# Attention decode with a gated FFN: K and V in four large units, K turned on VectorE

## The chip, the cores and the metric

The kernel runs on one core of a Trainium2 chip. The time is that of the device, in microseconds, from the first to the last instruction of the core; the median of the timed runs counts. The engines are TensorE (PE), VectorE (DVE), ScalarE (ACT), GpSimd (POOL) and SyncE (SP, which here only issues transfers). PEld is PE's loading of the stationary operand.

## What is computed

Two sequences of one token each (B = 2), model width 448, 16 query heads over 8 K/V heads of 256, and a window of the last 2048 keys of a cache of 8192:

```python
def reference(A_x, A_k_cache, A_v_cache, A_wq, A_wo, B_x, B_w1, B_w2):
    xn = _layernorm(A_x)                                  # [2, 1, 448]
    q = (xn @ wq) -> [2, 16, 1, 256]                      # wq 448 x 4096
    k, v = last W = 2048 rows of the caches, each head used by 2 query heads
    p = softmax(q k^T / 16);  o = p v                     # per sequence and head
    s = o -> [2, 1, 4096] @ wo                            # wo 4096 x 448
    g = silu(relu(xn @ w1) @ w2)                          # w1 448 x 1792, w2 1792 x 448
    return A_x + s * g
```

All inputs are bfloat16. K and V of the windows are 33.55 MB, wq and wo 3.67 MB each, w1 and w2 1.61 MB each.

## The kernel before

A small scheduler, `_Prog`, keeps one list of operations for each engine. Every list is executed strictly in the order in which the operations were added; dependences become semaphore waits. `run` writes the lists out inside an `nc.Block`, one body for each engine.

K and V come in 16 pieces each: one K/V head of one sequence, `[128 partitions x 16 keys x 256]`, 1 MB with rows of 8 KB (`kv_src`, L178). The pieces of K rotate through 6 buffers and those of V through 8; all are issued on SP in the order of the list at L463 to L475, behind wq and ahead of w1, w2 and wo (five parts, L481). A pair k is one head for both sequences.

- `do_T` (L260): PE transposes a chunk of K in four 128x128 f32 products (two bf16 values to an f32) into PSUM (L268); DVE (L278) and ACT (L280) in turn copy it to `kt`.
- `do_S` (L282): the scores of a pair, 16 products of 512 columns, four side by side in column tiles of the array; the moving operand steps 4 bytes.
- `ch_max`, `ch_rmT`, `ch_bias`, `ch_exp`, `ch_Pt`, `ch_sum` (L298 to L337): the softmax of a pair; maxima and P are transposed on PE.
- `do_PV` (L339), `do_osb` (L353), `do_oT` (L359): P times V in 32 products of 256 columns a pair, scaling, and folding into `at_exp`.
- `do_q` (L374) computes q from wq (28 products) and spreads it into `qz`.
- `do_H`, `do_hT`, `do_F` (L397 to L429): the FFN; H is twice seven products of 448 columns, one after the other, `do_F` 56 products of 112 columns and the sigmoid.

The table `steps` (L437 to L461) puts the parts of the pairs into one another: while K of pair k is transposed, the softmax and PV of pairs k-1 and k-2 run. FFN and output come after all pairs (L485 on): 128 products with wo (L498), two DVE operations (L503, L505), and two stores side by side on SP and ACT (L507), with a wait for both on SP.

Of the kernel before, what the change touches and what calls it, by code (L numbers as in the profile page):

```python
# [22 lines left out]
class _Prog:  # L23


# [14 lines left out]
    def run(self, block):  # L40
# [5 lines left out]
        for e, ops in self.lists.items():  # L46
            sem, count = self.es.enter_context(self.nc.semaphore(f"s_{e}")), 0
            for o in ops:
                if o.dma:
                    n += 1  # L50
                    o.sem, o.value = self.es.enter_context(self.nc.semaphore(f"d_{n}")), 16
                elif o.needed:
                    count += 1
                    o.sem, o.value = sem, count
# [16 lines left out]
        for name, e in (("gpsimd", POOL), ("sync", SP), ("scalar", ACTE), ("vector", DVE), ("tensor", PE)):  # L71
            def body(eng, ops=self.lists[e]):
                emit(eng, ops)
            getattr(block, name)(body)


def bass_recurrent_scan__sliding_block_cached__dense_activation_relu__decode_kernel(
# [21 lines left out]
    NT = W // 128  # L99
    NPAIR = HKV  # L100
    NCH = 8
    SLOTS = 7
    NKB = 6
    NVB = 8
    NKT = 12
    NP = 3
    HC = HD // 2
    FC = DFF // 2
    WO_PARTS = [10, 10, 8, 2, 2]
    NCOL = D // 4  # L110

    es = contextlib.ExitStack()
    with es:
# [8 lines left out]
        def view(t, off, dims, n=128, p0=0, pstep=1):  # L122
            width = t.shape[1]
            return bass.AP(t, p0 * width + off, [[width * pstep, n]] + dims)

        ident = named("ident", [128, 128], BF)
        ident_f = named("ident_f", [128, 128], F32)
        one_f = named("one_f", [128, 1], F32)
        par8 = named("par8", [128, 8], F32)
        par2 = named("par2", [128, 2], F32)  # L130
        qmask = named("qmask", [128, 4], F32)
        fold = named("fold", [128, 32], BF)
        gsum = named("gsum", [128, 128], F32)
        x_sb = named("x_sb", [128, D], BF)
        xg = named("xg", [128, 9 * 128], BF)
# [5 lines left out]
        q_n = named("q_n", [128, 512], BF)  # L141
        qz = named("qz", [128, 16 * NPAIR], BF)
        h_n = named("h_n", [128, FC], BF)
        h_sb = named("h_sb", [128, 28], BF)
        x_c = named("x_c", [128, NCOL], BF)
# [4 lines left out]
        rm = [named(f"rm{i}", [128, 1], F32) for i in range(2)]  # L150
        mrow = [named(f"mrow{i}", [128, 128], F32) for i in range(2)]
        bias = [named(f"bias{i}", [128, 1], F32) for i in range(2)]
        e_sb = [named(f"e_sb{i}", [128, 512], BF) for i in range(2)]
        ssum = [named(f"ssum{i}", [128, 1], F32) for i in range(2)]
        rs = named("rs", [128, NPAIR], F32)
        pt = [named(f"pt{i}", [128, 64], BF) for i in range(NP)]
        o_sb = [named(f"o_sb{i}", [128, 512], BF) for i in range(2)]
        at_exp = named("at_exp", [128, 256], BF)
        at2 = named("at2", [128, 64], BF)
# [4 lines left out]
        kbuf = [named(f"kbuf{i}", [128, NT * DH], BF) for i in range(NKB)]  # L164
        vbuf = [named(f"vbuf{i}", [128, NT * DH], BF) for i in range(NVB)]
        kt = [named(f"kt{i}", [128, 1024], BF) for i in range(NKT)]

        tb = [psum(f"tb{i}", [128, 1024], BF) for i in range(3)]
        sbk = psum("sbk", [128, 512], F32)
        fbk = psum("fbk", [128, 512], F32)  # L170
        obk = [psum(f"obk{i}", [128, 512], F32) for i in range(2)]
        mb16 = psum("mbk", [128, 1024], BF)
        mbk = mb16[:, :].bitcast(F32).tensor

        def mbk_ap(lo, n, rows=128):
            return view(mbk, lo, [[1, n]], n=rows)

        def kv_src(c, cache):  # L178
            hkv, b = divmod(c, 2)
            return cache[b, hkv, SK - W:SK, :].rearrange("(p t) d -> p (t d)", t=NT)  # L180

        d_x = pr.dma(ACTE, x_sb[0:B, :], A_x[:, 0, :])
        p_xc = pr.op(POOL, lambda e: e.memset(x_c[:, :], 0.0))
        d_xc = [pr.dma(ACTE, view(x_c, 0, [[1, NCOL]], n=4, p0=b, pstep=32),
                       A_x[b, 0, :].rearrange("(i n) -> i n", i=4), [p_xc]) for b in range(B)]
        d_k, d_v = {}, {}
        last_T, last_PV = {}, {}

        wq_src = A_wq.rearrange("r (hf c) -> (r hf) c", hf=2).rearrange("(p s) c -> p (s c)", s=SLOTS)
        w1_src = B_w1.rearrange("r (hf c) -> (r hf) c", hf=2).rearrange("(p s) c -> p (s c)", s=SLOTS)  # L190
        w2_src = B_w2.rearrange("(hf p j) n -> p hf (j n)", hf=2, j=7)
        wo_src = A_wo.rearrange("(p j) n -> p (j n)", j=32)

        def load_k(c):
            d_k[c] = pr.dma(SP, kbuf[c % NKB][:, :], kv_src(c, A_k_cache), [last_T.get(c - NKB)])

        def load_v(c):
            d_v[c] = pr.dma(SP, vbuf[c % NVB][:, :], kv_src(c, A_v_cache), [last_PV.get(c - NVB)])

        load_k(0)  # L200
        load_k(1)
        d_wq = pr.dma(SP, wqo[:, 0:SLOTS * HC], wq_src)
        load_k(2)
        load_k(3)
# [5 lines left out]
        i1 = pr.op(POOL, lambda e: e.memset(ident_f[:, :], 0.0), [p_id])  # L210
        p_idf = pr.op(POOL, lambda e: e.affine_select(
            out=ident_f[:, :], in_=ident_f[:, :], compare_op=ALU.not_equal, fill=1.0,
            base=0, pattern=[[-1, 128]], channel_multiplier=1), [i1])
        p_one = pr.op(POOL, lambda e: e.memset(one_f[:, :], 1.0), [p_idf])
        p_mr = [pr.op(POOL, lambda e, t=t: e.memset(t[0:1, :], 0.0)) for t in mrow][-1]
        p_qz = pr.op(POOL, lambda e: e.memset(qz[:, :], 0.0), [p_one])

        a_z = [pr.op(ACTE, lambda e, t=t: e.memzero(t[:, :])) for t in (obk[0], sbk, obk[1], fbk)]  # L218

# [4 lines left out]
        a_sd = pr.op(ACTE, lambda e: e.activation(sd[0:B, 1:2], sd[0:B, 0:1], ACT.Sqrt), [v_ve])  # L224
        v_rs = pr.op(DVE, lambda e: e.reciprocal(rstd[0:B, :], sd[0:B, 1:2]), [a_sd])
        for e2 in range(2):
# [5 lines left out]
        v_par = pr.op(DVE, lambda e: e.tensor_reduce(  # L232
            out=par2[:, :], in_=view(ident, 0, [[1, 2], [2, 64]]), axis=AX.X, op=ALU.add), [p_id])
        v_par8 = pr.op(DVE, lambda e: e.tensor_copy(
            view(par8, 0, [[2, 4], [1, 2]]), view(par2, 0, [[0, 4], [1, 2]])), [v_par])
        v_qm = pr.op(DVE, lambda e: e.tensor_reduce(
            out=qmask[:, :], in_=view(ident, 0, [[32, 4], [1, 32]]), axis=AX.X, op=ALU.add))

        def fold_op(e):
            with nc.allow_low_precision("zeros and ones"):  # L240
                return e.tensor_reduce(out=fold[:, :], in_=view(ident, 0, [[1, 32], [32, 4]]), axis=AX.X, op=ALU.add)
        v_fold = pr.op(DVE, fold_op)
        v_gs = pr.op(DVE, lambda e: e.tensor_copy(
            view(gsum, 0, [[32, 4], [1, 32]]), view(fold, 0, [[0, 4], [1, 32]])), [v_fold])
# [5 lines left out]
        for s in range(SLOTS):  # L250
            m_xr = pr.op(PE, mm(mbk_ap(2 * s, 2), xg[0:B, 128 * s + 128:128 * s + 256], ident[0:B, 0:B], s == 0),
                         [v_xn, p_id])
        v_xr = pr.op(DVE, lambda e: e.tensor_tensor(
# [3 lines left out]
        evac, last_S, freed = {}, {}, set()  # L257
        st = {}

        def do_T(i):  # L260
            k, s = divmod(i, NCH)
            c = 2 * k + s // 4
            bank, src = tb[i % 3], kbuf[c % NKB]
            src_f, bank_f = src[:, :].bitcast(F32), bank[:, :].bitcast(F32)
            deps = [d_k[c], p_idf, evac.get(i - 3)]
            for n in range(4):
                lo = (4 * (s % 4) + n) * (DH // 2)
                o = pr.op(PE, lambda e, n=n, lo=lo: e.matmul(  # L268
                    bank_f[:, n * 128:(n + 1) * 128], lhsT=src_f[:, lo:lo + 128], rhs=ident_f[:, :],
                    start=True, stop=True, is_transpose=True), deps)  # L270
                deps = []
            last_T[c] = o
            if s % 4 == 3:
                freed.add((load_k, c))
            dst = kt[i % NKT]
            deps = [o, last_S.get(i - NKT)]
            if i % 2 == 0:
                evac[i] = pr.op(DVE, lambda e: e.tensor_copy(dst[:, :], bank[:, :]), deps)  # L278
            else:
                evac[i] = pr.op(ACTE, lambda e: e.activation(dst[:, :], bank[:, :], ACT.Copy), deps)  # L280

        def do_S(k, b):  # L282
            bank = sbk
            deps = [st["q"], a_z[1]] + ([st["exp", k - 1]] if b == 0 and k else [])
            for dhi in range(2):
                lhsT = qz[:, 16 * k + 8 * dhi + 4 * b:16 * k + 8 * dhi + 4 * b + 4]
                for i in range(4):
                    ch = NCH * k + 4 * b + i
                    o = pr.op(PE, mm(bank[32 * i:32 * i + 4, :], lhsT,
                                     view(kt[ch % NKT], dhi, [[2, 512]]),  # L290
# [250 lines left out]
```

## Time and profile before

| what | value |
|---|---|
| median of three runs | 115.5 us (115.26 to 115.77) |
| the profiled execution, its span | 115.7 us |
| PE busy, instructions | 85.0 us (73%), 990 products |
| DVE busy | 49.4 us (43%), 131 instructions |
| ACT busy | 44.4 us (38%) |
| DMA read from HBM | 44.11 MB, 381 GB/s over the span |
| mean granted TensorE clock | 0.852 |
| first wo product, last DVE operation, end | 109.5, 113.0, 115.7 us |

The profile lists busy time by engine; a row of 40 digits for each engine, one digit for each 2.89 us, in tenths of busy time; the clock that TensorE was granted; the chain of work that ended last; and groups of like instructions with their mean duration, in nanoseconds, and the idle time before them with what ended it. Busy time of an engine that nobody waits for costs nothing.

### The profile page before, as it was taken

Reading aid. Unit: us, or ns where it says so; the run is one execution under the profiler, and the core shown is the slowest. Engines: PE = TensorE matmul, PEld = TensorE weight load, DVE = VectorE, ACT = ScalarE, POOL = GpSimd, SP = SyncE. Lnnn points to the kernel's source line nnn. Section 1 sums busy time; section 2 is a strip of 40 time slices with the busy share of each in tenths; the row PEclk is TensorE's granted clock in tenths of the full one; section 3 lists DMA queues with packets and bytes.
Section 4 is the critical chain, followed back from the end, with each engine's and each line's share of the span. In section 5 each row is a group of like instructions: output and inputs, shape, how many; then the busy total and the mean of one; then the engine's idle time right before and its main releaser. Section 6 shows DMA issues by size and latency. Waiting matters only on the chain.

```text
span 115.7 us, 2285 instructions
## 1 busy us (share of the span) xinstructions
PE 85.0 (73%) x990; PEld 53.7 (46%) x990; DVE 49.4 (43%) x131; ACT 44.4 (38%) x57; POOL 1.9 (2%) x13
## 2 busy tenths in 40 slices
PE   0009946980499799759989966999998695886390
PEld 0009923650275465428556544756665342225280
DVE  2046424560027456523745742565575524113401
ACT  1951650668024834813384380348465010000000
POOL 6000000000000000000000000000000000000000
PEclk9999999997559999985999998599999955555559
DMA  2998989999999999999999999999999999999200
GB/s 60 428 486 387 476 374 428 422 425 416 419 428 422 414 431 416 414 422 425 416 408 433 414 419 428 414 419 431 416 411 433 435 409 411 421 422 389 73 6 3
DMA packets 5934, 44.26 MB, mean 383 GB/s; under 512 B 674, under 2 KB 932, under 8 KB 1316
## 3 DMA queue, kind: packets, MB, share of 16 engines
q1 hardware_dynamic: 5896, 44.11, 91.7%
q8 instruction: 8, 0.13, 0.5%
q14 instruction: 2, 0.02, 0.0%
q10 hardware_dynamic: 28, 0.00, 0.0%
HBM read 44.11 MB, written 0.00 MB: 381 GB/s over the span
## 4 chain that ended last, share of the span: by engine, by line
DMA 46%; PE 38%; DVE 6%; ACT 4%; issue 1%; POOL 1%; POOLq 0%
DMA kbuf<-in_A_k_cache_dram 46%; PE tb L268 13%; PE fbk L247 10%; PE obk L247 6%; PE sbk L247 3%; PE mbk L247 3%; PE mbk L325 2%; ACT L224 1%; ACT L218 1%; DVE xg L227 1%; DVE h_n L404 1%; ACT obk L218 1%; DVE o_sb L355 1%; DVE tmp L427 1%; DVE rm L299 1%
## 5 line engine op out<-in xcount | busy, mean ns | idle before, releaser
L268 PE MATMUL tb<-ident_f,kbuf 128*128 128x128 f32 x256 | 43.7, 307 | 9.8 <-DMA kbuf<-in_A_k_cache_dram 9.8
L280 ACT ACTIVATE kt<-tb 128x1024 bf16<-128x1024 bf16 x32 | 32.6, 1023 | 42.7 <-PE tb L268 42.7
L268 PEld LDWEIGHTS tb<-ident_f,kbuf 128*128 128x128 f32 x256 | 31.8, 158 | 17.5 <-DMA kbuf<-in_A_k_cache_dram 10.9
L278 DVE COPY kt<-tb 128x1024 bf16<-128x1024 bf16 x32 | 22.1, 689 | 23.6 <-PE tb L268 23.6
L247 PE MATMUL obk<-vbuf,pt 128*4 128x256 bf16 x256 | 13.7, 305 | 0.0
L247 PE MATMUL sbk<-kt,qz 128*4 128x512 bf16 x128 | 10.6, 410 | 0.1
L355 DVE TENSOR_SCALAR o_sb<-obk,rs 128x256 bf16<-128x256 f32 x16 | 7.5, 471 | 1.6 <-PE obk L247 1.6
L299 DVE TENSOR_REDUCE rm<-sbk 128x1 f32<-128x512 f32 x8 | 5.5, 692 | 6.0 <-PE sbk L247 6.0
L247 PEld LDWEIGHTS obk<-vbuf,pt 128*4 128x4 bf16 x256 | 4.5, 87 | 5.7 <-issue 3.5
L318 ACT ACTIVATE e_sb<-sbk,bias 128x512 bf16<-128x512 f32 x8 | 5.5, 683 | 3.7 <-DVE bias L314 3.7
L247 PE MATMUL mbk<-ident,xg 2*128 2x2 bf16 x7 | 0.3, 163 | 8.9 <-DVE xg L227 8.9
L247 PE MATMUL fbk<-w_sb,xr 128*4 128x448 bf16 x14 | 5.5, 573 | 0.7 <-DVE h_n L404 0.7
L424 ACT ACTIVATE ea<-fbk 128x112 f32<-128x112 f32 x1 | 0.3, 264 | 14.7 <-PE fbk L247 14.7
L247 PE MATMUL fbk<-wqo,at 128*2 128x112 bf16 x128 | 3.2, 298 | 1.8 <-DVE g_sb L428 1.8
L247 PEld LDWEIGHTS mbk<-ident,xg 2*128 2x128 bf16 x7 | 0.3, 101 | 8.9 <-DVE xg L227 8.9
L330 DVE COPY pt<-mbk 128x64 bf16<-128x64 bf16 x8 | 1.5, 192 | 6.4 <-PE mbk L325 6.4
L325 PE MATMUL mbk<-ident,e_sb 128*128 128x128 bf16 x32 | 4.0, 264 | 0.0
L247 PEld LDWEIGHTS mbk<-ssum,gsum 128*128 128x128 f32 x16 | 3.3, 258 | 1.2 <-DVE pt L330 1.0
L247 PEld LDWEIGHTS fbk<-wqo,at 128*2 128x2 bf16 x128 | 2.9, 124 | 2.1 <-DVE g_sb L428 2.1
L247 PE MATMUL mbk<-ssum,gsum 128*128 128x1 f32 x16 | 3.4, 281 | 0.6 <-DVE pt L330 0.6
L325 PEld LDWEIGHTS mbk<-ident,e_sb 128*128 128x128 bf16 x32 | 2.3, 114 | 2.8 <-DVE kt L278 1.3
L404 DVE TENSOR_SCALAR h_n<-fbk 4x448 bf16<-4x448 f32 x2 | 1.2, 612 | 5.4 <-PE fbk L247 5.4
(65 smaller groups left out, 48.7 us busy)
## 6 DMA issues: line engine op xcount, KB each, us to landing
kbuf<-in_A_k_cache_dram SPq DMA_DIRECT2D x16, 1024.0 KB, 24.5
vbuf<-in_A_v_cache_dram SPq DMA_DIRECT2D x16, 1024.0 KB, 25.5
wqo<-in_A_wq_dram SPq DMA_DIRECT2D x1, 3584.0 KB, 15.0
w_sb<-in_B_w_dram SPq DMA_DIRECT2D x2, 1568.0 KB, 25.9
wqo<-in_A_wo_dram SPq DMA_DIRECT2D x2, 1120.0 KB, 28.4
wqo<-in_A_wo_dram SPq DMA_DIRECT2D x1, 896.0 KB, 27.6
wqo<-in_A_wo_dram SPq DMA_DIRECT2D x2, 224.0 KB, 25.2
x_c<-in_A_x_dram ACTq DMA_DIRECT2D x2, 0.9 KB
```

Source lines behind the costliest of these rows:

```text
L218: a_z = [pr.op(ACTE, lambda e, t=t: e.memzero(t[:, :])) for t in (obk[0], sbk, obk[1], fbk)]
L224: a_sd = pr.op(ACTE, lambda e: e.activation(sd[0:B, 1:2], sd[0:B, 0:1], ACT.Sqrt), [v_ve])
L247: return lambda e: e.matmul(out_ap, lhsT=lhsT, rhs=rhs, start=start, stop=stop, skip_group_check=True, **kw)
L268: o = pr.op(PE, lambda e, n=n, lo=lo: e.matmul(bank_f[:, n * 128:(n + 1) * 128], lhsT=src_f[:, lo:lo + 128], rhs=ident_f[:, :], start=True ...
L278: evac[i] = pr.op(DVE, lambda e: e.tensor_copy(dst[:, :], bank[:, :]), deps)
L280: evac[i] = pr.op(ACTE, lambda e: e.activation(dst[:, :], bank[:, :], ACT.Copy), deps)
L299: st["rm", k] = pr.op(DVE, lambda e: e.tensor_reduce(out=rm[k % 2][:, :], in_=sbk[:, :], axis=AX.X, op=ALU.max), [st["S", k], st.get(("rmT ...
L318: st["exp", k] = pr.op(ACTE, lambda e: e.activation(e_sb[k % 2][:, :], sbk[:, :], ACT.Exp, bias=bias[k % 2][:, 0:1], accum_out=ssum[k % 2] ...
L325: o = pr.op(PE, lambda e, j=j: e.matmul(mb16[:, 512 + 128 * j:640 + 128 * j], lhsT=e_sb[k % 2][:, 128 * j:128 * j + 128], rhs=ident[:, :], ...
L330: st["pt", k] = st["mbk"] = pr.op(DVE, lambda e: e.tensor_copy(view(pt[k % NP], 0, [[16, 4], [4, 4], [1, 4]]), view(mb16, 512, [[128, 4], ...
L355: st["osb", k] = pr.op(DVE, lambda e: e.tensor_scalar(out=o_sb[k % 2][:, cols], in0=obk[k % 2][:, cols], scalar1=rs[:, k:k + 1], scalar2=N ...
L404: st["h_n"] = pr.op(DVE, lambda e: e.tensor_scalar(out=h_n[0:4, u * (FC // 2):(u + 1) * (FC // 2)], in0=fbk[0:4, 0:FC // 2], scalar1=0.0, ...
```

## The change

K and V come in four units u, one for each sequence b and each half hg of the eight heads: 4 heads, `[128 partitions x 64 keys x 256]`, 4.19 MB in one DMA with rows of 32 KB. Partition 4p + g holds 64 consecutive keys of head g. There are two buffers each for K and V. wq is issued first, then K and V of units 0 and 1; K of unit u + 2 is issued behind S of unit u, V of unit u + 2 behind PV of unit u, then w1, w2 and wo, all on SP.

K is turned in place by DVE in 32x32 blocks of f32 (two bf16 values each), in four instructions of 2048 columns a unit. S works on the turned K within each group of 32 partitions, with a q that is zero but for its own group (`qstat`). The maxima are turned on DVE instead of PE; P is turned on DVE, spread by 16 products with a permutation, and masked so that each partition's head meets its own V. PV is 64 products of 256 columns a unit. `do_out` folds the result into `at2` with eight products.

The FFN is computed after the last unit with column tiles (H 28 products, F 14), its result folded by four f32 products to 8 rows (sequence and quarter of the columns). wo's first 24 row groups go into column tiles of a bank of their own and are folded in likewise, the last 8 straight into the 8 rows. x is loaded in that form by one DMA, and the output is one store. The engines' lists are written out without a block.

```diff
-        for name, e in (("gpsimd", POOL), ("sync", SP), ("scalar", ACTE), ("vector", DVE), ("tensor", PE)):
-            def body(eng, ops=self.lists[e]):
-                emit(eng, ops)
-            getattr(block, name)(body)
+        for eng, e in ((nc.sync, SP), (nc.gpsimd, POOL), (nc.scalar, ACTE), (nc.vector, DVE), (nc.tensor, PE)):
+            emit(eng, self.lists[e])
...
-    WO_PARTS = [10, 10, 8, 2, 2]
+    NT = 64
+    NU = 4
+    WO_PARTS = [16, 8, 4, 2, 2]
+    WO_TILED = 24
...
+        def kv_src(u, cache):
+            b, hg = divmod(u, 2)
+            return cache[b, 4 * hg:4 * hg + 4, SK - W:SK, :].rearrange("g (p t) d -> p g (t d)", t=NT)
...
+        def load_k(u):
+            d_k[u] = pr.dma(SP, kb[u % 2][:, :], kv_src(u, A_k_cache), [last_S.get(u - 2)])
+
+        def load_v(u):
+            d_v[u] = pr.dma(SP, vb[u % 2][:, :], kv_src(u, A_v_cache), [last_PV.get(u - 2)])
+
         d_wq = pr.dma(SP, wqo[:, 0:SLOTS * HC], wq_src)
-        load_k(2)
-        load_k(3)
+        for u in range(2):
+            load_k(u)
+            load_v(u)
...
+        v_q = pr.op(DVE, lambda e: e.tensor_scalar(
+            out=view(q_x, 0, [[256, 8], [128, 2], [1, 32]]), in0=view(qbk, 0, [[64, 8], [1, 2], [2, 32]]),
+            scalar1=SCALE, scalar2=None, op0=ALU.mult), [m_q])
+        v_qx = pr.op(DVE, lambda e: e.tensor_copy(
+            view(q_x, 32, [[128, 16], [32, 3], [1, 32]]), view(q_x, 0, [[128, 16], [0, 3], [1, 32]])), [v_q])
+        deps = [v_qx, st["mbk"]]
+        for n in range(16):
+            m_qt = pr.op(PE, mm(mbk[:, 16 * n:16 * n + 16], q_x[:, 128 * n:128 * n + 128],
+                                view(ident, 0, [[32, 4], [1, 4]]), n == 0), deps)
+            deps = []
+        for Q in range(4):
+            st["q"] = st["mbk"] = pr.op(DVE, lambda e, Q=Q: e.tensor_copy(
+                qstat[32 * Q:32 * Q + 32, 256 * Q:256 * Q + 256], mbk[32 * Q:32 * Q + 32, 0:256]), [m_qt, p_z])
+
+        def do_turn(u):
+            kf = kb[u % 2][:, :].bitcast(F32)
             for n in range(4):
+                st["turn", u] = pr.op(DVE, lambda e, n=n: e.transpose(
+                    kf[:, 2048 * n:2048 * n + 2048], kf[:, 2048 * n:2048 * n + 2048]), [d_k[u]])
+
+        def do_S(u):
+            b, hg = divmod(u, 2)
+            deps = [st["turn", u], st["q"], z(sbk), st.get(("exp", u - 1))]
+            for jp in range(8):
+                j, par = divmod(jp, 2)
+                for g in range(4):
+                    o = pr.op(PE, mm(sbk[32 * g:32 * g + 8, :],
+                                     view(qstat, jp * 16 + 4 * g + 2 * hg + b, [[128, 8]]),
+                                     view(kb[u % 2], 64 * j + 2 * g + par, [[DH, NT], [8, 8]]),
+                                     jp == 0, jp == 7, tile_position=(0, 32 * g)), deps)
                     deps = []
+            last_S[u] = o
+
+        def do_soft(u):
+            v = pr.op(DVE, lambda e: e.tensor_reduce(
+                out=rm[:, 0:1], in_=sbk[:, :], axis=AX.X, op=ALU.max), [last_S[u], p_z, st.get(("rmt", u - 1))])
+            v = st["rmt", u] = pr.op(DVE, lambda e: e.transpose(rm_t[:, :], rm[:, :]), [v])
+            v = pr.op(DVE, lambda e: e.tensor_reduce(
+                out=view(bt, 0, [[2, 4], [1, 2]]), in_=view(rm_t, 0, [[0, 4], [1, 2], [2, 4]]),
+                axis=AX.X, op=ALU.max, negate=True), [v, p_z, st.get(("bias", u - 1))])
+            v = st["bias", u] = pr.op(DVE, lambda e: e.transpose(bias[:, :], bt[:, :]), [v, st.get(("exp", u - 1))])
+            st["exp", u] = pr.op(ACTE, lambda e: e.activation(
+                e_sb[:, :], sbk[:, :], ACT.Exp, bias=bias[:, 0:1], accum_out=ssum[:, 0:1]),
+                [v, st.get(("et", u - 1)), st.get(("gs", u - 1))])
+            st["et", u] = pr.op(DVE, lambda e: e.transpose(e_t[:, :], e_sb[:, :]),
+                                [st["exp", u], st.get(("sp", u - 1))])
+
+        def do_spread(u):
+            deps = [st["et", u], v_perm, st.get(("pt", u - 1))]
+            for t4 in range(4):
+                for Q in range(4):
+                    o = pr.op(PE, mm(spk[32 * Q:32 * Q + 32, 32 * t4:32 * t4 + 32],
+                                     perm[:, 32 * t4:32 * t4 + 32],
+                                     view(e_t, 2 * Q, [[32, 16], [1, 2]]),
+                                     True, True, tile_position=(0, 32 * Q)), deps)
+                    deps = []
...
+            st["pt", u] = pr.op(DVE, lambda e: e.tensor_tensor(
+                out=view(pt[u % 2], 0, [[8, 64], [2, 4], [1, 2]]), in0=view(spk, 0, [[2, 64], [0, 4], [1, 2]]),
+                in1=view(pmask, 0, [[0, 64], [1, 4], [0, 2]]), op=ALU.mult), [o, v_pm, last_PV.get(u - 2)])
...
+        def do_PV(u):
+            bank, p, v = obk[u % 2], pt[u % 2], vb[u % 2]
+            deps = [d_v[u], st["pt", u], z(bank), st.get(("osb", u - 2))]
+            for n in range(NT):
+                t4, tb = divmod(n, 16)
+                t, i = 4 * tb + t4, n % 4
+                o = pr.op(PE, mm(bank[32 * i:32 * i + 8, 0:DH], p[:, 8 * n:8 * n + 8], v[:, t * DH:t * DH + DH],
+                                 n < 4, n >= NT - 4, tile_position=(0, 32 * i)), deps)
+                deps = []
+            last_PV[u] = o
+
+        def do_out(u):
+            b, hg = divmod(u, 2)
+            st["osb", u] = pr.op(DVE, lambda e: e.tensor_scalar(
+                out=o_sb[:, :], in0=obk[u % 2][:, 0:DH], scalar1=rs[:, u:u + 1], scalar2=None, op0=ALU.mult),
+                [last_PV[u], st["rs", u], st.get(("oT", u - 1))])
...
+            st["at"] = st["mbk"] = pr.op(DVE, lambda e: e.tensor_copy(
+                view(at2, 3 + 4 * b, [[11, 32]], n=64, p0=lo), mbk[lo:lo + 64, 288:320]), [o, p_z])
...
+        for u in range(NU):
+            do_turn(u)
+            do_S(u)
+            do_soft(u)
+            do_spread(u)
+            if u + 2 < NU:
+                load_k(u + 2)
+            do_PV(u)
+            if u + 2 < NU:
+                load_v(u + 2)
+            do_out(u)
+
+        st["w1"] = pr.dma(SP, w1_sb[:, :], w1_src)
+        st["w2"] = pr.dma(SP, w2_sb[:, :], w2_src)
...
+        do_H()
+        do_F()
+
+        deps = [st["at"], z(wbk)]
+        for j in range(WO_TILED):
+            i = j % 4
+            o = pr.op(PE, mm(wbk[32 * i:32 * i + B, 0:D], view(at2, 11 * j + 3, [[4, 2]]), wqo[:, j * D:j * D + D],
+                             j < 4, j >= WO_TILED - 4, tile_position=(0, 32 * i)), deps + [landed.get(j)])
+            deps = []
+        v_wc = pr.op(DVE, lambda e: e.tensor_copy(wc[:, :], wbk[:, 0:D]), [o])
...
+        for j in range(WO_TILED, 28):
+            direct(j, j == WO_TILED, [landed.get(j), st["g"]])
+        deps = [v_wc]
+        for i in range(4):
+            pr.op(PE, mm(fbk[0:8, 0:NCOL], bsel[:, 3 - i:11 - i], wc[:, NCOL * i:NCOL * i + NCOL], False), deps)
+            deps = []
+        for j in range(28, 32):
+            m_o = direct(j, False, [landed.get(j)])
+
...
+        d_o = pr.dma(SP, out.rearrange("b s (i n) -> (b s i) n", i=4), out_sb[0:8, :], [v_o])
+        pr.op(SP, None, [d_o])
+
+        pr.run()
```

In the tail, `do_H` is 28 products of 448 columns into four column tiles, a ReLU out of PSUM and one DVE turn of 448 columns; `do_F` is 14 products of 448 columns, a copy to SBUF, four f32 products that fold it to 8 rows, and the sigmoid as before on those rows; `direct(j)` is four products of 112 columns.

## The prediction

> **What bounds the kernel now.** I read the page's 40 slices first, then the chain that ended last, then the windows by stage, then the groups.
>
> The slices: the DMA row stands at 9 from slice 4 to 36, at some 420 GB/s, and falls only in the last three.
>
> ```profile
> PE   0009946980499799759989966999998695886390
> DVE  2046424560027456523745742565575524113401
> PEclk9999999997559999985999998599999955555559
> DMA  2998989999999999999999999999999999999200
> ```
>
> So transfers set the end up to about 107.5 us (37 slices of 2.89 us); the remaining 8 us are a tail of products, sigmoid and store. The chain says so too: its largest share is a K load, and PE's share is mostly work right after a landing and the tail.
>
> ```profile
> DMA 46%; PE 38%; DVE 6%; ACT 4%; issue 1%; POOL 1%; POOLq 0%
> ```
>
> The windows (span; busy time and count of PE, PEld, DVE, ACT, POOL; granted clock; DMA share; GB/s) hold the two facts I use most.
>
> ```profile
> 7.50:10.00 2.50, 1.12 (x11) 1.11 (x12) 2.40 (x9) 0.00 (x0) 0.00 (x0) 1.00 1.17 505
> ...
> 40.00:60.00 20.00, 17.46 (x186) 10.96 (x186) 10.17 (x26) 9.35 (x13) 0.00 (x0) 0.91 1.01 418
> ```
>
> ```profile
> 92.20:95.70 3.50, 3.17 (x42) 1.66 (x40) 1.06 (x6) 0.78 (x2) 0.00 (x0) 0.50 0.98 408
> 98.10:104.50 6.40, 5.60 (x16) 1.49 (x16) 0.84 (x3) 0.00 (x0) 0.00 (x0) 0.50 1.03 429
> ```
>
> First: bytes per busy share. With 8 KB rows it is 418/1.01 = 414 GB/s; in the window where wq's 28 KB rows moved it is 505/1.17 = 432. Second: once the full-width transposes of L268 stop at 88 us, the clock falls to 0.50 and stays there, though PE is 90% busy with narrow products.
>
> The groups that give durations:
>
> ```profile
> L247 PE MATMUL sbk<-kt,qz 128*4 128x512 bf16 x128 | 10.6, 410 | 0.1
> L299 DVE TENSOR_REDUCE rm<-sbk 128x1 f32<-128x512 f32 x8 | 5.5, 692 | 6.0 <-PE sbk L247 6.0
> L318 ACT ACTIVATE e_sb<-sbk,bias 128x512 bf16<-128x512 f32 x8 | 5.5, 683 | 3.7 <-DVE bias L314 3.7
> L278 DVE COPY kt<-tb 128x1024 bf16<-128x1024 bf16 x32 | 22.1, 689 | 23.6 <-PE tb L268 23.6
> ```
>
> **What goes.** The 256 K transposes of L268 (43.7 us of PE) and their evacuation (22.1 us of DVE, 32.6 of ACT) are worth nothing in themselves: they run under the loads, the cover being the 9s of the DMA row. What they also do is hold PE's clock up.
>
> **Loads.** The bytes stay the same. K and V (33.55 MB) come in 8 DMAs of 4.19 MB with 32 KB rows; wq's 28 KB row is the near one, so 432 GB/s: 9.7 us a load, 77.7 us for eight, against 81.0 at 414. The transfers gain 3.3 us (bounds 0 and 3.3). The schedule: in the trace wq was issued at 1.64, landed 15.0 us later, and 2.1 MB of K lay ahead of it: 16.6 - 5.1 - 8.5 = 3.05 us until data flows. Now wq is first: lands at 11.5, K0 at 21.3, V0 31.0, K1 40.7, V1 50.4, K2 60.1, V2 69.8, K3 79.5, V3 89.2, w1 and w2 (3.8 each, as now) 96.8, wo (3.67 MB at about 420) 105.5.
>
> On SP four new waits stand: K2 behind S of unit 0, V2 behind PV 0, K3 behind S 1, V3 behind PV 1; behind each all later loads queue, w1, w2 and wo among them. By the sum below these come at 34, 42, 56 and 64 us, while the queue runs dry only at 50.4, 60.1, 69.8 and 79.5. They cost nothing while units take less than about 29 us.
>
> **The chain of one unit.** DVE's list is strictly in order: the four turns of unit u+1 stand behind o_sb and the at2 copy of unit u, these behind PV, PV behind P, P behind S, S behind the turns. So nothing of one unit overlaps the next; a unit is a sum.
>
> - Turn, 4 x [128 x 2048 f32] on DVE. No such operation is in the trace. DVE rows with f32 input go at one element per 1.04 ns: 112 elements 275 ns (L503), 512 elements 692 (L383); so 2.29 us each, 9.2 for four, 9.0 with the 0.05 us by which consecutive DVE instructions overlap. The other bound is the L278 copy, two 2-byte elements per cycle: 1024 in 689, so 1.22 each, 4.9 for four. I take 9.0: f32 is the nearer row.
> - S, 32 products of 512 columns, four side by side. At the half clock a column is 0.835 ns (L247's first FFN product, 448 columns every 374 ns in the 0.50 window). 32 x 512 / 4 x 0.835 = 3.4, plus 0.2 to drain: 3.6. At full clock 1.9 (q now: 28 such products started in 1.3 us).
> - Max 0.69, two small transposes and a reduction of 0.2 each, gaps: 1.45. Exp 0.68 with its accumulator read 0.20 and gap: 0.95. P turned, 512 elements: 0.7.
> - Spread, 16 products of 32 columns. Small products of w2 took 26 ns each (56 in 1.48 us), the 128-wide L325 ones 150 (4 in 0.61): 0.6 to 2.5; 0.7 taken, as these are narrow. Times mask, 512 from PSUM: 0.75.
> - PV, 64 products of 256 columns: 3.4 + 0.2 = 3.6 (now 16 take 1.02 at 0.50); 1.9 at full clock.
> - o_sb 0.47, 8 small products 0.45, copy 0.2, gaps: 1.25.
>
> Sum 22.0 us, against 19.4 between K landings. Which clock? The low one. A unit gives PE some 8.5 us of narrow products in two bursts and leaves it idle through 9 us of turning; in the trace the idle stretch 26 to 30 us put the clock to 0.50 from 27.3 to 34.1, and 1.8 us of idleness near 49 did it at 51.6.
>
> [...]
>
> **The q part** at the start gains products and copies on PE and DVE (28 products at half clock 3.4, copies 0.7 and at most 1.7, 16 products about 2, four copies of 0.47): wq's 11.5 + 9.7 = 21.2, just when K0 lands. I cost it at nothing; without that cover each us is a us on unit 0.
>
> **The tail, behind unit 3.** H, 28 products of 448: 2.8. ReLU 0.67, turn 0.67. F, 14 products: 1.6. Copy 0.67. Four f32 fold products of 112 columns: 0.6 (one pass) to 1.7 (four); 1.0 taken. Then the sigmoid (0.27, 0.22, 0.85, 0.27, gaps: 1.75) beside 24 products of wo (2.44); wo's end is later: 3.44 after the copy, its evacuation to 4.16, four more fold products 5.1, 16 small ones 5.6, the two DVE ends of 0.28 6.2, the store as now (113.33 to 115.7) 8.6. Together 6.4 + 8.6 = 15.0. Of wo's parts all have landed (105.5), so "FFN under wo's first parts" hides nothing.
>
> **No block, one store.** SP's waits at L511 are 0.2 and 0.3 us; the two stores of now are issued side by side. Bounds 0 to 0.5 gained; 0 taken.
>
> **The sum.** 21.3 + 4 x 22.0 = 109.3, less 0.25 as H needn't wait for the last copy, plus 15.0 = 124.0 us, against the profiled 115.7 (the median is 115.5, nothing to correct). Its own range is 118 (units of 20.5, where some bursts reach the high clock) to 130 (spread at its upper bound).
>
> **Rivals.**
> 1. The chain fits between the loads (chance 0.25): units under 19.4 us. Either the turns run at the copy's rate (unit 17.9: 79.5 + 17.9 + 15.0 = 112.4), or PE holds the full clock (S and PV 1.9 each, unit 18.3, tail 12: 79.5 + 18.3 + 12 = 109.8). Transfers alone would give 105.5 + 3.4 = 108.9, the 3.4 being 8 products, two DVE ends and the store. It decides from 19.4 us a unit on. For: q ran at 1.00 after an idle 1.3 us. Against: the 0.50 of all narrow work from 92 us on.
> 2. S reads too slowly (0.15): its moving operand now steps 16 bytes within K; today's steps 4, and took 410 ns a product against 379 for q's unit step (8%, partly clock). At half rate a unit is 25.6 and the time 21.3 + 102.4 + 14.8 = 138.5; halfway, 131. [...]
> 3. The loads get slower (0.04): adjacent partitions now read rows 4 MiB apart. At half of 432 GB/s, 11.5 + 155 puts V3 at 166.8, and the end near 186.
>
> That the load order doesn't do what it says isn't one: the four waits above have 9 us of slack or more.
>
> **How the numbers follow.** Forecast 0.52 (118 to 130), rival 1 0.25 (108.5 to 115), between them, within 0.5% of now, 0.04, rival 2 0.15 (131 to 139), rival 3 0.04. Faster by over 0.5% is rival 1, slower all but the 0.04; 0.5% is about what these runs can tell from nothing. Both signs have weight, so beside the forecast's own 118 to 130 stands the range 109.5 to 134: it leaves out some 0.08 of rival 2, 0.04 of rival 3 and 0.05 below.
>
> **What would show it.** Turns of 2.2 us each with nothing of another unit under them; PE's clock at 0.50 from 30 us on; S 3.6 and PV 3.6; the DMA row finished near 105 and the last 15 us without loads. It is wrong if a unit's period is 19.4 (the K landings), if turns take 1.2, or if the clock is 1.00 in S.

## The result, and the profile after

The changed kernel takes 138.9 us (median; the kernel before 115.5): 1.203 times as long, 95% interval 1.196 to 1.210. Some executions of either kernel are slower, at a lower mean clock, both profiled ones among them (spans of 140.7 us here and 115.7 before); the others, which alone count for times and ratios, have spans of 137.3 to 138.6 and 112.3 to 114.0, and where a whole time is meant spans are compared below with 137.5. The time is about 1.3 us more than the span here, and about 1.8 us more in the kernel before.

The 40 slices of the changed kernel (3.52 us each):

```profile
PE   0006300039819101991840079356005954882794
...
DVE  3600528960160898005159920343993034116251
...
PEclk9999955555995955698555557977755896555559
DMA  5999999999999999999999999899980000000000
```

The transfers end close to where they were forecast, at about 106 us (105.5 was the forecast; the last load counts as landed at 107.3), and some 35 us without loads follow. PE and DVE take turns: where one has a 9, the other has a 0. That is the strictly serial unit. The chain, by engine and by line, has changed owner:

```profile
PE 42%; DVE 38%; DMA 14%; ACT 2%; issue 1%; SPq 0%
DVE kb L281 25%; PE sbk L246 21%; DMA kb<-in_A_k_cache_dram 14%; PE obk L246 10%; PE fbk L246 4%; PE mbk L246 2%; ACT e_sb L305 2%; DVE e_t L308 2%; DVE rm L298 2%; DVE pt L323 2%; PE qbk L246 2%; PE wbk L246 2%; DVE h_n L363 1%; DVE o_sb L341 1%; PE spk L246 1%
```

From 46% the loads have gone to 14%, and that is K0 alone. On top stand the turns (25%) and S (21%). One unit of the chain, and S of the last unit (start, duration, what):

```profile
47.00 8.71 DVE kb L281 x4
...
55.75 7.62 PE sbk L246 x30
...
63.39 0.70 DVE rm L298
...
67.62 3.61 PE obk L246 x49
...
71.25 0.49 DVE o_sb L341
...
72.77 8.90 DVE kb L281 x4
...
106.97 7.57 PE sbk L246 x26
```

A unit is 25.8 us here, 25.4 in the one before: turn 8.7, S 7.6, softmax 4.3, PV 3.6, the rest 1.5. All lie within 0.3 us of the sum on record but S, for which it had 3.6. The groups:

```profile
L246 PE MATMUL sbk<-kb,qstat 128*8 128x512 bf16 x128 | 30.2, 1088 | 41.2 <-DVE kb L281 41.2
L281 DVE STREAM_TRANSPOSE kb<-kb 128x2048 f32<-128x2048 f32 x16 | 35.5, 2275 | 3.0 <-DMA kb<-in_A_k_cache_dram 3.0
L298 DVE TENSOR_REDUCE rm<-sbk 128x1 f32<-128x512 f32 x4 | 2.8, 692 | 30.6 <-PE sbk L246 30.6
...
L305 ACT ACTIVATE e_sb<-sbk,bias 128x512 bf16<-128x512 f32 x4 | 2.8, 688 | 106.1 <-DVE bias L304 106.1
...
L363 DVE TENSOR_SCALAR h_n<-qbk 128x448 bf16<-128x448 f32 x1 | 2.1, 2079 | 2.4 <-PE qbk L246 2.4
```

A product of S no longer takes 410 ns but 1088, and with 7.5 us for 32 products, four side by side, a set of four takes 0.94 on average. One DVE row surprises too: the FFN's ReLU, 2.08 us for 448 columns. The windows of unit 0 (span; busy time and count of PE, PEld, DVE, ACT, POOL; granted clock; DMA share; GB/s) are the turn, three pieces of S, and PV:

```profile
21.60:30.40 8.80, 0.00 (x0) 0.00 (x0) 8.80 (x4) 0.00 (x0) 0.00 (x0) 0.50 1.01 436
30.50:32.50 2.00, 1.98 (x12) 0.37 (x16) 0.00 (x0) 0.00 (x0) 0.00 (x0) 0.50 0.91 393
32.50:34.50 2.00, 2.00 (x12) 0.35 (x8) 0.00 (x0) 0.00 (x0) 0.00 (x0) 0.50 1.18 508
...
36.50:38.00 1.50, 1.50 (x8) 0.00 (x0) 0.00 (x0) 0.00 (x0) 0.00 (x0) 1.00 1.11 481
42.20:45.70 3.50, 3.38 (x64) 2.11 (x64) 0.00 (x0) 0.00 (x0) 0.00 (x0) 0.56 1.04 449
```

In S twelve products start in 2 us at a clock of 0.50, and eight in 1.5 us at 1.00: the clock doubles, and they start no faster. So S isn't limited by the array; that something feeds it too slowly is the guess that the experiments test. The loads aren't it: S of the last unit takes the same 7.57 us from 107.0 on, where the DMA row is at 0. PV, at 0.56, is on its 3.4.

### The profile page after: what moved, and what is told of

Read it like the earlier page. It is cut to its first block, busy times and chain, and to the rows that moved or that the text cites. A ratio compares the mean times of both kernels' runs of the same rounds, so it can differ in the third digit from the quotient of the medians.

```text
span 140.7 us, 1473 instructions
## 1 busy us (share of the span) xinstructions
PE 64.5 (46%) x653; PEld 25.9 (18%) x653; DVE 61.8 (44%) x83; ACT 9.0 (6%) x18; POOL 2.2 (2%) x12
## 4 chain that ended last, share of the span: by engine, by line
PE 42%; DVE 38%; DMA 14%; ACT 2%; issue 1%; SPq 0%
DVE kb L281 25%; PE sbk L246 21%; DMA kb<-in_A_k_cache_dram 14%; PE obk L246 10%; PE fbk L246 4%; PE mbk L246 2%; ACT e_sb L305 2%; DVE e_t L308 2%; DVE rm L298 2%; DVE pt L323 2%; PE qbk L246 2%; PE wbk L246 2%; DVE h_n L363 1%; DVE o_sb L341 1%; PE spk L246 1%
## 5 line engine op out<-in xcount | busy, mean ns | idle before, releaser
L246 PE MATMUL sbk<-kb,qstat 128*8 128x512 bf16 x128 | 30.2, 1088 | 41.2 <-DVE kb L281 41.2
L281 DVE STREAM_TRANSPOSE kb<-kb 128x2048 f32<-128x2048 f32 x16 | 35.5, 2275 | 3.0 <-DMA kb<-in_A_k_cache_dram 3.0
L246 PEld LDWEIGHTS sbk<-kb,qstat 128*8 128x8 bf16 x128 | 5.2, 107 | 58.9 <-DVE kb L281 41.6
L246 PE MATMUL obk<-vb,pt 128*8 128x256 bf16 x256 | 13.9, 408 | 1.9 <-DVE rs L326 1.9
L246 PEld LDWEIGHTS obk<-vb,pt 128*8 128x8 bf16 x256 | 8.6, 123 | 6.0 <-issue 2.1
L305 ACT ACTIVATE e_sb<-sbk,bias 128x512 bf16<-128x512 f32 x4 | 2.8, 688 | 106.1 <-DVE bias L304 106.1
L341 DVE TENSOR_SCALAR o_sb<-obk,rs 128x256 bf16<-128x256 f32 x4 | 1.9, 484 | 14.4 <-PE obk L246 14.4
L246 PE MATMUL qbk<-wqo,xr 128*4 128x512 bf16 x28 | 3.0, 601 | 5.7 <-DMA wqo<-in_A_wq_dram 5.7
L308 DVE STREAM_TRANSPOSE e_t<-e_sb 128x512 bf16<-128x512 bf16 x4 | 2.8, 711 | 3.4 <-ACT e_sb L305 3.4
L323 DVE TENSOR_TENSOR pt<-spk,pmask 128x512 bf16<-128x512 f32 x4 | 2.8, 692 | 1.7 <-PE spk L246 1.7
L363 DVE TENSOR_SCALAR h_n<-qbk 128x448 bf16<-128x448 f32 x1 | 2.1, 2079 | 2.4 <-PE qbk L246 2.4
L246 PE MATMUL wbk<-wqo,at 128*2 128x448 bf16 x24 | 3.0, 574 | 0.0
```

The lines of the kernel that those rows point to most:

```text
L246: return lambda e: e.matmul(out_ap, lhsT=lhsT, rhs=rhs, start=start, stop=stop, skip_group_check=True, **kw)
L281: st["turn", u] = pr.op(DVE, lambda e, n=n: e.transpose(kf[:, 2048 * n:2048 * n + 2048], kf[:, 2048 * n:2048 * n + 2048]), [d_k[u]])
L305: st["exp", u] = pr.op(ACTE, lambda e: e.activation(e_sb[:, :], sbk[:, :], ACT.Exp, bias=bias[:, 0:1], accum_out=ssum[:, 0:1]), [v, st.get ...
L308: st["et", u] = pr.op(DVE, lambda e: e.transpose(e_t[:, :], e_sb[:, :]), [st["exp", u], st.get(("sp", u - 1))])
L323: st["pt", u] = pr.op(DVE, lambda e: e.tensor_tensor(out=view(pt[u % 2], 0, [[8, 64], [2, 4], [1, 2]]), in0=view(spk, 0, [[2, 64], [0, 4], ...
L341: st["osb", u] = pr.op(DVE, lambda e: e.tensor_scalar(out=o_sb[:, :], in0=obk[u % 2][:, 0:DH], scalar1=rs[:, u:u + 1], scalar2=None, op0=A ...
```

## The experiments

All edits are against the changed kernel; `...` stands for lines left out, and in a line the rest of a call.

**e1_steps: the step of S's moving operand, one value for each unit.** The scores of units 1 to 3 are not the reference's.

```diff
-  view(kb[u % 2], 64 * j + 2 * g + par, [[DH, NT], [8, 8]])
+  view(kb[u % 2], 64 * j + 2 * g + par,
+       ([[DH, NT], [8, 8]], [[4, 512]], [[2, 512]], [[1, 512]])[u])
```

> S of unit 0 reads K as the changed kernel does (16 bytes from one column to the next), unit 1 steps 8 bytes, unit 2 4 bytes, unit 3 2 bytes; the scores of units 1 to 3 are therefore not the reference's. All else is as it was, the 8-column stationary included. Theory A (S pays for each 16-byte line that its moving operand opens): S 7.5 us in unit 0, about 3.6 in units 2 and 3, and unit 1 tells where the price begins (3.6 if two columns a line are enough, some 5.5 if each line costs). Theory B (the strided stationary, the 8 output rows or the hand-over from VectorE makes S slow): 7.5 us in all four. Theory C (four streams that read the same lines at once): 7.5 in units 0 to 2 at least, since neighbours still lie 4 bytes apart.

The timeline of PE, S of units 0 to 3 (start, duration):

```profile
30.53 7.60 PE L246 MATMUL sbk<-kb,qstat 128*8 128x512 bf16 x32 [13.47 <-DVE kb L281]
...
56.27 3.85 PE L246 MATMUL sbk<-kb,qstat 128*8 128x512 bf16 x32 [9.08 <-DVE kb L281]
...
78.13 3.38 PE L246 MATMUL sbk<-kb,qstat 128*8 128x512 bf16 x32 [9.31 <-DVE kb L281]
...
99.66 3.60 PE L246 MATMUL sbk<-kb,qstat 128*8 128x512 bf16 x32 [9.08 <-DVE kb L281]
```

16 bytes 7.60, 8 bytes 3.85, 4 bytes 3.38, 2 bytes 3.60. The price is there with one column in each 16 bytes. By the start times in the trace a set of four starts every 0.43 us at 4 and at 2 bytes and every 0.45 at 8, all at a clock of 0.50; the 3.38 is less than the 3.60 because its last products run at 1.00. Whether the price is gone with two columns in 16 bytes or only halved, this run can't tell: 3.85 at a clock of 0.50 is a little above the 3.60 at the same clock, and it is also half of 7.60. At that clock the array alone needs some 3.4 us for S (32 x 512 / 4 x 0.835 ns), which would hide a halved price of 3.8 almost wholly. No run steps 8 bytes at the full clock. The kernel before stepped 4 bytes in S and 2 in q (ns, least, median and most):

```profile
L247 PE MATMUL sbk<-kt,qz x128: 385/387/632, 20.2 to 89.9; 128*4 128x512 bf16 x128
...
L247 PE MATMUL obk<-wqo,xr x28: 377/379/379, 16.7 to 18.0; 128*4 128x512 bf16 x28
```

Both medians are of products at a clock of 1.00. A set of four starts there every 0.226 us at 4 bytes and every 0.216 at 2; at 16 bytes it was 0.90. A quarter of 0.90 is 0.225, so a price for every 16 bytes that are read fits all of these; that is an estimate from them and not shown, and no run shows by what a slow read comes about.

Theory B falls: the stationary operand, the output rows and the hand-over from DVE are the same in all four units of e1_steps. C falls too, as the four streams lie 4 bytes apart in unit 1 (3.85 us) as in unit 0 (7.60); e2_streams tests it directly.

**e2_streams: where the streams lie, and how many there are.** Scores not the reference's.

```diff
+  col = 0 if u == 3 else g
+  off, dims = ((2 * g + par, [[16, 512]]), (4096 * g + par, [[8, 512]]),
+               (64 * j + par, [[DH, NT], [8, 8]]), (64 * j + 2 * g + par, [[DH, NT], [8, 8]]))[u]
...
-  tile_position=(0, 32 * g)
+  tile_position=(0, 32 * col)
```

> Again only S's moving operand differs, so the scores are not the reference's: unit 0 steps 32 bytes; unit 1 16 bytes with the four column tiles' streams 8 KB apart; unit 2 16 bytes with all four streams on the same addresses; unit 3 as in the changed kernel, but all 32 products in one column tile, so one stream at a time. Theory A: 7.5 us in units 0, 1 and 2 (a line a column, wherever it lies); in unit 3 the stream alone tells whether the price is per stream: 32 x 0.94 = 30 us if it is, 32 x 0.43 = 13.7 us at the half clock if four streams share one port. Theory C: unit 1 3.6 us, unit 2 7.5 or more.

The timeline of PE again:

```profile
30.61 7.52 PE L246 MATMUL sbk<-kb,qstat 128*8 128x512 bf16 x32 [13.50 <-DVE kb L281]
...
55.87 7.49 PE L246 MATMUL sbk<-kb,qstat 128*8 128x512 bf16 x32 [9.08 <-DVE kb L281]
...
80.99 7.61 PE L246 MATMUL sbk<-kb,qstat 128*8 128x512 bf16 x32 [9.31 <-DVE kb L281]
...
106.64 27.67 PE L246 MATMUL sbk<-kb,qstat 128*8 128x512 bf16 x32 [9.08 <-DVE kb L281]
```

A step of 32 bytes costs what 16 does; streams 8 KB apart (7.49) and streams on the same addresses (7.61) cost the same. One stream at a time needs 27.67 / 32 = 0.86 us a product, hardly less than the 0.94 that four need together. So each stream pays for itself, 0.86 us / 512 = 1.7 ns a column, and the column tiles hardly compete. That is the price of theory A for one column in each 16 bytes, and C, which asked for 3.6 us in unit 1, is refuted.

**e5_step4: S at 4 bytes in all units**, scores not the reference's.

```diff
-  view(kb[u % 2], 64 * j + 2 * g + par, [[DH, NT], [8, 8]])
+  view(kb[u % 2], 64 * j + 2 * g + par, [[2, 512]])
```

> S steps 4 bytes in all four units (scores not the reference's), the rest as it was. Theory A, that the missing term of the prediction is S's read alone: S 3.6 us, a unit 25.4 - 3.9 = 21.5, the time 137.5 - 4 x 3.9 = 122 us, next to the 124.0 of the prediction. If the clock or something that grows with the unit is behind it, the other parts move too and the time stays above 128.

123.07 us, 1.072 (1.064 to 1.081) of the kernel before; the span is 121.8, that is 15.7 under 137.5, or 3.9 for each unit. The chain has in unit 1

```profile
43.35 8.71 DVE kb L281 x4
...
52.11 3.63 PE sbk L246 x32
```

so the turn is as it was and S alone has shrunk. The units start 21.6 us apart (21.57, 21.62 and 21.54 from S to S), 3.9 less than before; nothing else in them moves with it.

**e4_tail: the block back, and the ReLU's write in order.**

```diff
-  out=view(h_n, 0, [[1, 32], [32, 14]]), in0=view(qbk, 0, [[14, 32], [1, 14]]),
+  out=view(h_n, 0, [[32, 14], [1, 32]]), in0=view(qbk, 0, [[1, 14], [14, 32]]),
...
-  pr.run()
+  with nc.Block() as block:
+      pr.run(block)
```

> Two parts of the tail alone: the block is back around the engines' lists, and the ReLU writes h_n in order (and reads PSUM at a step of 56 bytes) instead of writing every 64 bytes. If the strided write made the 2.08 us, the ReLU takes 0.65 and 1.4 us go; if a strided side costs either way, it stays near 2. The block: from the last VectorE operation to the end 1.3 us without it; with it 2.4 if the block was the difference to the kernel before, 1.3 if it was the second store. Time: 137.5 - 1.4 + 1.1 = 137.2 if both hold.

The group of the ReLU:

```profile
L365 DVE TENSOR_SCALAR h_n<-qbk 128x448 bf16<-128x448 f32 x1 | 0.6, 625 | 2.4 <-PE qbk L248 2.4
```

625 ns against 2079: the strided write into SBUF made the difference, the strided read from PSUM costs nothing here (the copy of as many columns from PSUM, in order on both sides, takes 0.62 us in the same tail). From the end of the last DVE operation to the end of the span it is 137.84 to 139.5, 1.7 us, with the block; 1.3 without it; 2.4 in the kernel before, which has the block and two stores. So neither expectation holds alone: about 0.4 goes with the block, by one run, and the other 0.7 with what else differs at the end of the kernel before, the second store or its queue; which of the two, no run separates. The times of all its executions (137.41 to 141.28; the changed kernel had 138.62 to 142.05) overlap; no verdict on the whole is drawn from them.

**e3_quarters: S behind each turn.** Nothing is left out.

```diff
-  st["turn", u] = pr.op(DVE, ...
+  st["turn", u, n] = pr.op(DVE, ...
...
+  for n in range(4):
+      deps = [st["turn", u, n], st["q"], z(sbk), st.get(("exp", u - 1))]
       for jp in range(8):
...
-  mm(sbk[32 * g:32 * g + 8, :], ..., view(kb[u % 2], 64 * j + 2 * g + par, [[DH, NT], [8, 8]]), ...
+  mm(sbk[32 * g:32 * g + 8, 128 * n:128 * n + 128], ...,
+     view(kb[u % 2], 4096 * n + 64 * j + 2 * g + par, [[DH, 16], [8, 8]]), ...
```

> Nothing is left out; S is cut into four quarters of 128 columns, each behind its own turn instruction, so that three of the four run under the next turn. Theory A (S costs 1.8 ns a column and stream, its place decides what it costs the unit): a quarter takes 7.5 / 4 = 1.9 us, less than a turn's 2.2, so only the last shows: a unit 25.4 - 5.6 = 19.8 us, close to the 19.4 between K's landings, and the span 21.6 + 4 x 19.8 + 17.0 - 0.3 = 117.5, the time 119. Rival: 128 small products cost by their number (0.11 us for each weight load), so a quarter takes over 2.2 us and a unit 20.5 or more: 122 us.

117.45 us, 1.017 (1.003 to 1.031) of the kernel before, span 115.9. The timeline of unit 0:

```profile
21.78 8.89 DVE L281 STREAM_TRANSPOSE kb<-kb 128x2048 f32<-128x2048 f32 x4 [2.81 <-DMA kb<-in_A_k_cache_dram]
...
24.15 2.02 PE L246 MATMUL sbk<-kb,qstat 128*8 128x128 bf16 x32 [6.93 <-DVE kb L281]
...
26.34 6.45 PE L246 MATMUL sbk<-kb,qstat 128*8 128x128 bf16 x96 [0.17 <-DVE kb L281]
...
32.84 0.69 DVE L299 TENSOR_REDUCE rm<-sbk 128x1 f32<-128x512 f32 x1 [2.16 <-PE sbk L246]
```

S's first quarter starts 2.4 us into the turns, and the maximum (32.84) comes 2.2 us behind their end (30.67), where it came 7.6 behind. A quarter takes 2.0, where a fourth of 7.5 is 1.9: the number of products costs next to nothing. The price a column is still paid; it is under the turns.

**e6_early: the FFN ahead of the end as well.** On top of e3_quarters; the lines with # tell in words what is moved:

```diff
+  # loads: K2, V2, K3, w1, w2, V3, wo
+  # PE, last unit: S, H, spread, F, PV, fold of PV, fold of F, wo
+  # DVE: first turn of unit u + 1, o_sb and at2 copy of unit u, three more turns
+  # the products into fbk wait for F's copy, no longer for the sigmoid
-  v = pr.op(DVE, lambda e: e.tensor_copy(zc[:, :], fbk[:, 0:D]), [o])
+  st["zc"] = pr.op(ACTE, lambda e: e.activation(zc[:, :], fbk[:, 0:D], ACT.Copy), [o])
```

> Nothing is left out. On top of the quarters: the first turn of a unit goes ahead of o_sb and the at2 copy of the one before; w1 and w2 are loaded ahead of the last V; H runs behind the last S, F ahead of the last PV, ReLU and copy on ScalarE, the sigmoid beside wo's products. By theory A the chain is then bound by the landing of K3 (79.5 to 80): 9.0 + 1.9 + 4.2 puts P at 95, V3 lands at 97, PV to 100.5, out 102, wo's products to 107.5, two VectorE ends and a store of 1.3 us: span 109.5, time 111, about 4% under the kernel before. If something else still stands in the chain (the fold products, the at2 copy behind a turn, F waiting for w2), 112 to 116.

114.07 us, 0.984 (0.979 to 0.989). The "112 to 116" of the expectation came, for three reasons that the chain shows:

```profile
42.17 2.20 issue
44.37 0.45 DVE o_sb L342
...
45.52 0.30 DVE at L352
...
94.82 2.09 ACT h_n L364
96.91 0.52 ACT e_sb L306 x2
...
100.04 1.50 PE fbk L246 x13
101.54 3.32 PE obk L246 x59
```

Behind the first turn DVE waits for PE's fold before the at2 copy (44.82 to 45.52) and only then turns on; the strided ReLU, now on ScalarE, takes its 2.09 there too and holds exp up until 96.9; and PV waits until 101.5 behind F, though V3 landed at 99.0.

**e7_order: these three orders changed.** Again the lines with # tell it in words:

```diff
+  # DVE: turn 0 of u + 1, o_sb of u, turn 1, at2 copy of u, turns 2 and 3
+  # ACT: exp, then the ReLU, written in order
+  # PE, last unit: S, H, spread, PV, F, fold of PV, wo's column tiles, fold of F
```

> Nothing is left out. Three orders are changed against e6_early: the at2 copy goes between the second and the third turn of the next unit (in e6_early VectorE stood 1.1 us between the first turn and the copy, waiting for TensorE's fold); the ReLU goes behind the last exp on ScalarE and writes in order (it held exp up by 1.6 us there); F goes behind the last PV and its fold products behind wo's column tiles. If these three are what stands in the chain, 112.7 - 1.1 - 1.6 - 1.4 = 108.6 us of span, 110 us of time, 4 to 5% under the kernel before. If the landing of wo's last parts decides, the end comes 3 us behind it and little is gained: 112 us.

112.11 us, 0.976 (0.972 to 0.981), the fastest here. Nothing is left out. The end of its chain:

```profile
62.80 42.32 DMA wqo<-in_A_wo_dram
...
105.17 0.55 PE wbk L246 x8
...
106.47 2.35 PE fbk L246 x40
...
109.14 0.26 DVE out_sb L461
```

From 62.8 to 105.1 the chain is wo's load: the transfers set the end here. What follows (105.1 to 110.7) is the rest of the tail, with wo's last part landing at 107.4 (108.9 in the kernel before). 108.6 was not reached, the expectation's second case (112) was.

## Why the prediction was wrong

Its direction and its serial unit hold, its time does not: 124.0 on record, range 109.5 to 134, measured 138.9.

- **The step that failed** is the S term of the unit, "32 x 512 / 4 x 0.835 = 3.4, plus 0.2 to drain: 3.6". It measured 7.5 to 7.6, in each of four units: 4 x 3.95 = 15.8 us more, where the whole span is 13.5 above the 124.0. About 2.3 came back elsewhere, from the other parts of the units and from the tail. The term was priced by array time from rows whose moving operand steps 2 and 4 bytes; the changed S steps 16, and then pays 1.7 to 1.9 ns a column and stream instead. e5_step4 takes that step away and lands at 121.8 us of span.
- **Time and span.** The 124.0 is a sum of span, set against a span of 115.7 and a time of 115.5 as if these were one ("nothing to correct"). The time is 1.3 us longer than the span, which the sum doesn't hold.
- **Rival 2** had the place, nearly the price (7.2 us at half rate) and the sum (138.5), and was given 0.15. No row of before shows a half rate; the runs showed 7.5 to 7.6 us for S. That its sum comes so close is partly luck: S cost 0.3 us a unit more than that, the rest less. The row read as evidence against it, 410 ns a product at 4 bytes against 379 at 2, says nothing of 16 bytes, where e1_steps shows twice the time of 8. Bounds of S that the trace of before left open should have been carried into the range, as was done for the turns; the range ended at 134, in the middle of this rival.
- **The serial unit** was right: the slices alternate, and a unit's other parts are 17.9 against the 18.4 summed.
- **The turns**: 2275 ns each, 8.7 to 8.9 for four, against 9.0. Rival 1's turns at the copy's rate, 4.9 for four, are refuted.
- **The clock**: 0.50 in most of the turns and of PV, as forecast. S reaches 1.00 in its second half, which the prediction had named as a sign of being wrong; it came, but not with what rival 1 made of it: S gains nothing by it (four products start every 0.90 us at either clock), and where S is short, in e5_step4, the clock is at 0.50 in all of S of the last unit (3.60 us; the window from 94 to 100 us).
- **Loads**: K0 landed at 21.55 (21.3), the last load at 107.3 (105.5). The queue's share times the span is 0.737 x 140.7 = 103.7 us, and 103.7 to 104.0 in the other seven runs with these loads, against 0.917 x 115.7 = 106.1 in the one trace of before: some 2.2 of the 3.3 us came. The four waits on SP cost nothing: the DMA share is 0.99 to 1.02 in the windows from 22 to 100 us. Rival 3 is refuted: 436 GB/s in the first window.
- **The tail** took 17.1 us in the profiled execution, from 123.6, against 15.0, at a clock of 0.50 until near the end: H alone took 2.74 us. In e5_step4 and e3_quarters, with the same tail, the clock is 1.00 in H and F, H takes 1.45, and the tail 14.0 and 14.1. In all three the ReLU takes 1.4 more than on record (a strided write priced by an unstrided row) and the end 1.1 less than 2.4. The f32 fold products were put at 1.0 between 0.6 and 1.7, the author's estimate, which no row of before shows; at a clock of 0.50 the first four took 1.65 (131.62 to 133.27, eight products in the trace).
- **What bounds the kernel before.** The prediction read the chain of before as set by transfers up to 107.5. Its last load ends earlier:

```profile
44.43 25.84 DMA kbuf<-in_A_k_cache_dram
70.27 0.04 issue
70.31 0.66 PE tb L268 x4
```

From 70.3 us on the chain holds no load; it is mostly PE's work on the pairs, then the tail. The DMA engines are as busy meanwhile (a share of 1.01 from 60 to 100 us), so both lie close together, and which of them a change would have to shorten first the trace alone doesn't show.

## What to carry to other kernels

A product's price had two sides here: columns by the clock (3.4 us for S at 0.50), and how its moving operand lies in memory (7.5 to 7.6 us with a step of 16 bytes). When a change alters an access pattern, look at its step before pricing it by a row of the same shape, and if no row has that step, carry both ends into the range. Where a slow step can't be avoided, cut the work so that it starts with the first piece of its input: here that was worth 5.5 us a unit with one loop, more than the step itself cost.

## What the runs showed of the hardware that was not expected

- A moving operand with one 2-byte column in each 16 bytes is read at 1.8 to 1.9 ns a column for four streams side by side, the same at clock 0.50 and 1.00, at 32 bytes, and with the streams on the same addresses, 4 bytes or 8 KB apart (7.49 to 7.62 us for S), and at 1.7 for one stream. With 8 bytes and less, S took 3.4 to 3.9 us at about the half clock, where the array alone needs some 3.4 by its 0.835 ns a column.
- VectorE's and ScalarE's writes of 448 columns with a step of 64 bytes took 2.08 and 2.09 us, in order 0.63 and 0.53; the reads from PSUM at a step of 56 bytes in the latter cost nothing that shows (copies in order on both sides took 0.62 and 0.54).
- K and V in 8 loads of 32 KB rows took some 2.2 us less transfer time than in 32 loads of 8 KB rows, of 106; the row and the number of loads weren't separated.
